# Two moves in a hand-ordered attention and GLU kernel: the last two memory reads of a segment, and the second-half query relays of the first segment

## The chip, the cores and the metric

The kernel runs on one core of one Trainium2 chip. A core has five engines that run side by side and meet through semaphores: TensorE (PE, matmuls; PEld is its weight loader), VectorE (DVE), ScalarE (ACT), GpSimd (POOL) and SyncE (SP), which here only issues transfers. Transfers run on 16 DMA engines. Matmul results go to PSUM, a small memory from which DVE or ACT must copy them out; POOL can't read it.

The metric is device time in microseconds (us), the median of three runs. One execution was also profiled; its trace gives every instruction's start and length.

## The reference

An input x of 2048 rows by 640 columns is normalized by rows. One branch is attention with 32 heads of 20 columns in four segments of 512 rows. Inside a segment it is causal softmax attention; a memory M of all segments before it is read with phi(q) and then updated with phi(k) and v. The other branch is a gated feed-forward layer. The result is x + s * silu(feed-forward).

```python
xn = _layernorm(x, axis=-1)
for s in range(N):                       # N = 4 segments of L = 512 rows
    logits = einsum('bhqd,bhkd->bhqk', qs, ks) * scale + mask
    a_dot = einsum('bhqk,bhkd->bhqd', softmax(logits), vs)
    pq = phi(qs)
    num = einsum('bhld,bhde->bhle', pq, M)
    den = einsum('bhld,bhd->bhl', pq, z)[..., None] + 1e-06
    o = g * (num / den) + (1.0 - g) * a_dot
    pk = phi(ks)
    M = M + einsum('bhld,bhle->bhde', pk, vs)
    z = z + einsum('bhld->bhd', pk)
s = concat(o) @ wo
h = sigmoid(xn @ w_gate) * (xn @ w_up)
return x + s * silu(h @ w_down)
```

## The kernel before

**Segments and slots.** After a start-up part, the kernel goes through the four segments. A segment has 20 slots: 4 pairs of head groups by 5 units of score tiles. A slot begins with its score matmuls (`scores`, L522, into Sps); ACT turns them into weights pt by an exponential over 128 x 2048 (L527), POOL masks the diagonal (L530), and a slot or two later PE multiplies pt with the values (`weigh`, L547, into Aps). Between these fixed pieces PE gets other work: the value, key and query products of the next segment (`v_tile` L360, `k_chunk` L289, `q_chunk` L321), the gate, up and down products (L428, L438, L456), the output product of the segment before (`o_proj`, L502), the memory update (`m_update`, L388) and the memory reads.

**A planner at build time.** All engines' orders are written out by this Python code; nothing is reordered later. `at(time, cost, fn)` puts a task into a heap, due at a time counted in slots, with a planned PE cost in us. A task of a cost over 0.1 goes to `tasks`, others to `soft`. Each slot has two fills: the first runs tasks that are due before now + 0.45, the second tasks and soft work due before now + 1.0. In both, feed-forward work (`bulk`) is handed out as far as the slot's budget goes, which is a common level less the planned costs of the tasks in the slot. R is 20/24 = 0.833 slots, a unit of many due times; w is the first slot of a segment.

**PSUM tiles.** Everything on PE but scores and attention output takes its PSUM tile from one pool, `ps_d`, with three tiles. A matmul group can begin when the tile that it takes over has been copied out by DVE or ACT.

**A memory read** (`mem_read`, L402 to L420) is three matmuls from phi(q) in q5 and the memory in Mbd into a tile am (L410), and then three DVE steps that empty it: the denominator (L415, rm), its reciprocal (L417) and the product into om (L418). There are eight in each segment from the second on: row block `i // 2` by column half `i % 2`. They are due from L671, the memory's update of the same segment from L664.

**Transfers and SP's queue.** SP issues its transfers in the recorded order and waits in place for what each needs. Their completions are counted on eight semaphores in turn, so that a transfer also waits until the eighth before it has landed. Queries and keys of a segment are first written out to DRAM (Qs, Ks) and then *relayed* back in the layout of the scores, head by head (`relay`, L274, four transfers for a half of the heads, into KT and QT). The *bound* of the logits, Cs, goes the same way into four more rows of QT (`c_in`, L353, four transfers for a half). The second half of the heads is first used in slot 10. In the first segment these relays are recorded in the start-up part (L630 to L632). There too the planner gets the normalization of the next segment's last two row blocks (`ln_norm`, L626 and L627: DVE makes xn, and SP transposes it into xnT by a transfer, L263). Value products with these blocks are due from slot 5 on (L649). Phi of the keys is transposed by SP into pkt (L378), which the memory update reads.

Of the kernel before, what the change touches and what calls it, by code (L numbers as in the profile page):

```python
# [55 lines left out]
R = NSLOT / 24  # L56
# [3 lines left out]
def kernel(  # L60
# [30 lines left out]
    Qs = [dpool.tile([D, L], BF, name=f"Qs{i}") for i in range(2)]  # L91
# [11 lines left out]
    def at(time, cost, fn, *a):  # L103
        count[0] += 1
        heapq.heappush(first if fn is phi else tasks if cost > 0.1 else soft, (time, count[0], cost, fn, a))
# [80 lines left out]
    QT = [cpool.tile([P, 4, L], BF, name=f"QT{i}") for i in range(3)]  # L186
# [5 lines left out]
    def v_ones(a, b):  # L192
        for i in range(a, b):
            nc.gpsimd.memset(V[i][:, :, DH:VW], 1.0)
# [32 lines left out]
    def ln_stats(n, p, i0=0, i1=2):  # L227
        s = st[n]
        x = s[f"x{p}"]
        if i0 == 0:  # L230
            s[f"mv{p}"] = lnp.tile([P, 2, 2], F32, name="mv")
            s[f"rstd{p}"] = lnp.tile([P, 2], F32, name="rstd")
        mv, rstd = s[f"mv{p}"], s[f"rstd{p}"]
        for i in range(i0, i1):
            bs = lnp.tile([P, 2, 6], F32, name="bs")
            nc.vector.bn_stats(bs[:, 0, :], x[:, i, 0:HB])
            nc.vector.bn_stats(bs[:, 1, :], x[:, i, HB:D])
            nc.vector.bn_aggr(mv[:, i, :], bs[:])

        def root():  # L240
            nc.gpsimd.tensor_scalar(rstd[:, i0:i1], mv[:, i0:i1, 1], EPS, None, op0=ALU.add)
            nc.gpsimd.tensor_tensor(rstd[:, i0:i1], rstd[:, i0:i1], nhalf[:, i0:i1], op=ALU.pow)
        if n <= 1:
            root()
        else:
            later(0.6, root)

    def ln_norm(n, p, i):
        s = st[n]
        if "xnT" not in s:  # L250
            s["xnT"] = xpool.tile([P, DC, L], BF, name="xnT")
        xn = lnp.tile([P, D], BF, name="xn")
        nc.vector.tensor_scalar(xn[:], s[f"x{p}"][:, i, :], s[f"mv{p}"][:, i, 0:1], s[f"rstd{p}"][:, i:i + 1],
                                op0=ALU.subtract, op1=ALU.mult)
        j = 2 * p + i
        dst = s["xnT"][:, :, j * P:(j + 1) * P]
        if n == 0:
            pT = dtile([P, DC, P], BF, "pT")
            for c in range(DC):
                nc.tensor.transpose(pT[:, c, :], xn[:, c * P:(c + 1) * P], ident[:])  # L260
            nc.scalar.copy(dst, pT[:])
        elif n == 1:
            nc.sync.dma_start_transpose(dst, xn[:])  # L263
        else:
            later(0.7, lambda: nc.sync.dma_start_transpose(dst, xn[:]))


    def half_tile(tiles, n, half):
        return tiles[(2 * n + half) % 3]

    def relay(n, half, src, dst):
        rows = src[n % 2].rearrange("(g r d) n -> r d g n", r=4, d=DH)
        for r in range(4):
            nc.sync.dma_start(half_tile(dst, n, half)[32 * r:32 * r + DH, :, :], rows[r][:, 4 * half:4 * half + 4, :])  # L274
# [33 lines left out]
    def stage_out(n, half, src, dst, name):  # L308
        a, b = ((0, 3), (3, 5))[half]
        nc.sync.dma_start(src[n % 2][a * P:b * P, :].rearrange("(c p) n -> p c n", p=P), st[n][name][:, a:b, :])  # L310
        if n:
            later(1.0, relay, n, half, src, dst)
# [36 lines left out]
    def c_in(n, halves=(0, 1)):  # L349
        rows = Cs[n % 2].rearrange("b (g r) n -> r b g n", r=4)  # L350
        for half in halves:
            for r in range(4):
                nc.sync.dma_start(half_tile(QT, n, half)[32 * r + DH:32 * r + KR, :, :],  # L353
                                  rows[r][:, 4 * half:4 * half + 4, :])

    def v_tile(n, j, half):
        s = st[n]
        ps = dtile([P, HB], F32, "psv")
        for k in range(DC):
            nc.tensor.matmul(ps[:], lhsT=s["xnT"][:, k, j * P:(j + 1) * P],  # L360
                             rhs=W["v"][:, k, half * HB:(half + 1) * HB],
                             start=(k == 0), stop=(k == DC - 1))
        va = V[4 * (n % 2) + j]
        evacuate(va[:, half * 16:(half + 1) * 16, 0:DH], ps[:].rearrange("p (h e) -> p h e", e=DH))
# [203 lines left out]
    def warm(count):  # L568
        ps = dtile([P, L], F32, "wps")
        for i in range(count):  # L570
            nc.tensor.matmul(ps[:, 0:P], lhsT=ident[:], rhs=ident[:], start=True, stop=True)

    def startup():
        warm(WARM)
        nc.gpsimd.memset(KT[0][:], 1.0)
        ln_stats(0, 0, 0, 1)
        ln_stats(0, 0, 1, 2)
        ln_norm(0, 0, 0)
        warm(10)
        ln_stats(0, 1, 0, 1)  # L580
        ln_norm(0, 0, 1)
        v_tile(0, 0, 0)
        ln_stats(0, 1, 1, 2)
        v_tile(0, 1, 0)
        ln_norm(0, 1, 0)
        v_tile(0, 0, 1)
        ln_norm(0, 1, 1)
        v_tile(0, 2, 0)
        v_tile(0, 1, 1)
        v_tile(0, 2, 1)  # L590
        v_ones(0, 4)
        make_ind()
        nc.gpsimd.memset(KT[1][:], 1.0)
        for c in range(DC):
            k_chunk(0, c)
        nc.gpsimd.memset(KT[2][:], 1.0)
        stage_out(0, 0, Ks, KT, "k5")
        for c in range(DC):
            q_chunk(0, c)
            if c == 0:  # L600
                stage_out(0, 1, Ks, KT, "k5")
                relay(0, 0, Ks, KT)
            elif c == 2:
                stage_out(0, 0, Qs, QT, "q5")
            if c < 2:
                ln_stats(1, 0, c, c + 1)
        make_bd()
        v_ones(4, 8)
        take(1)
        q_bound(0)  # L610
        relay(0, 0, Qs, QT)
        stage_out(0, 1, Qs, QT, "q5")
        c_in(0, (0,))
        load_glu(1, 0)
        load_glu(1, 1)
        ln_stats(1, 1, 0, 1)
        gates()
        take(1)
        ln_norm(1, 0, 0)
        ln_norm(1, 0, 1)  # L620
        take(1)
        ln_stats(1, 1, 1, 2)
        take(5)
        at(0.1, 0.68, v_tile, 0, 3, 0)
        at(0.5, 0.68, v_tile, 0, 3, 1)
        at(R * 2.0, 0.0, ln_norm, 1, 1, 0)  # L626
        at(R * 2.3, 0.0, ln_norm, 1, 1, 1)  # L627
        load_glu(2, 0)
        load_glu(2, 1)
        relay(0, 1, Ks, KT)  # L630
        relay(0, 1, Qs, QT)
        c_in(0, (1,))  # L632

    startup()
    at(7.5, 0, load_late, "d", B_w_down)
# [3 lines left out]
    for n in range(NSEG):  # L639
        w = NSLOT * n  # L640
        m = n + 1
        if m < NSEG:
            if n:
                for p in range(2):
                    for i in range(2):
                        at(w + (-1.4, -0.7, 0.1, 0.55)[2 * p + i], 0.1, ln_stats, m, p, i, i + 1)
                        at(w + (0.6, 0.9, 1.7, 2.0)[2 * p + i], 0.1, ln_norm, m, p, i)
            for i in range(8):
                at(w + R * (3.5 + (0.6 * i if i < 4 else 2.5 + 0.55 * (i - 4))), 0.68, v_tile, m, i // 2, i % 2)  # L649
            for c in range(DC):  # L650
                at(w + R * (8.8 + 1.0 * c if n else 9.4 + 0.9 * c), 1.08, k_chunk, m, c)
                at(w + R * (13.8 + 1.1 * c), 1.08, q_chunk, m, c)
                if m + 1 < NSEG:
                    at(w + R * (12.8 + 0.85 * c), 0.0, phi, m, "k5", c)
                at(w + R * (17.4 + 0.8 * c), 0.0, phi, m, "q5", c)
            at(w + R * 19.2, 0.6, q_bound, m)
            if m + 1 < NSEG:
                for p in range(2):
                    at(w + R * (16.1 + p), 0.0, x_load, m + 1, p)
            if n == 0:  # L660
                for c in range(DC):
                    at(R * (2.6 + 0.8 * c), 0.0, phi, 0, "k5", c)
            for i, cs in enumerate(([0, 1, 2], [3, 4])):
                at(w + (9.05, 11.0)[i], 0.75 - 0.25 * i, m_update, n, cs)  # L664
        if n >= 1:
            for j in range(4):
                at(w + R * (1.1 + 0.3 * j), 0.0, o_ready, n - 1, j)
                at(w + R * (4.0 + 0.5 * j if j < 3 else 9.6), 0.0, xr_load, n - 1, j)
            for i in range(8):
                at(w + R * (5.4 + 1.1 * i), 0.68, o_proj, n - 1, i // 2, i % 2)  # L670
                at(w + R * (3.4 + 0.85 * i), 0.25, mem_read, n, i // 2, i % 2)  # L671

    for j in range(4):
        at(NSLOT * NSEG - 8 + 0.5 * j, 0.0, xr_load, NSEG - 1, j)
# [71 lines left out]
    n = NSEG - 1  # L746
# [39 lines left out]
```

## Time and profile before

| What | us |
|---|---|
| median of three runs | 339.26 |
| lowest and highest of them | 338.82, 339.61 |
| the profiled execution | 337.32 |
| its span, from first to last instruction | 335.6 |
| mean granted TensorE clock in it | 1.0 of full speed |

| Work | How often | Busy us | Mean ns |
|---|---|---|---|
| exponential of the scores, ACT L527 | 80 | 150.1 | 1876 |
| mask, POOL L530 | 80 | 77.1 | 963 |
| gate matmuls, PE L428 | 240 | 59.6 | 379 |
| up matmuls, PE L438 | 240 | 59.7 | 379 |
| down matmuls, PE L456 | 384 | 57.1 | 299 |
| attention output, PE L547 | 1280 | 44.5 | 173 |
| output product, PE L502 | 160 | 25.9 | 300 |

The profiled execution gives every duration used below; the time of a run holds a little more than the span. Busy time is no measure of what sets the end: an engine that is off the chain may idle or be busy at no cost. The matmuls' ends are modelled, so that they seem to overlap; the time from the start of one group of matmuls to the start of the next is the better measure. In a timeline a line is a group of instructions: its start, its length, engine, line, operation, what it writes and reads, how many; in brackets the idle time of that engine ahead of it and who ended it.

### The profile page before, as it was taken

Reading aid. Unit: us, or ns where it says so; the run is one execution under the profiler, and the core shown is the slowest. Engines: PE = TensorE matmul, PEld = TensorE weight load, DVE = VectorE, ACT = ScalarE, POOL = GpSimd, SP = SyncE. Lnnn points to the kernel's source line nnn. Section 1 sums busy time; section 2 is a strip of 40 time slices with the busy share of each in tenths; the row PEclk is TensorE's granted clock in tenths of the full one; section 3 lists DMA queues with packets and bytes.
Section 4 is the critical chain, followed back from the end, with each engine's and each line's share of the span. In section 5 each row is a group of like instructions: output and inputs, shape, how many; then the busy total and the mean of one; then the engine's idle time right before and its main releaser. Section 6 shows DMA issues by size and latency. Waiting matters only on the chain.

```text
span 335.6 us, 8361 instructions
## 1 busy us (share of the span) xinstructions
PE 328.0 (98%) x3402; PEld 186.1 (55%) x3402; DVE 224.0 (67%) x532; ACT 226.1 (67%) x237; POOL 111.6 (33%) x157
## 2 busy tenths in 40 slices
PE   7999999999999999999999999999999999999995
PEld 6544455555664565644565466554556665544673
DVE  6376366589868677688756978885663687543365
ACT  3653897788876675477686775566887776786730
POOL 6645222323236222332233523242222323223214
PEclk9999999999999999999999999999999999999999
DMA  7956984674811621135620461142220620210032
GB/s 234 328 196 198 288 105 85 230 226 117 205 57 36 123 80 41 49 117 120 189 72 2 61 142 56 47 152 68 72 70 3 93 76 32 76 43 3 2 62 78
DMA packets 54725, 35.53 MB, mean 106 GB/s; under 512 B 28576, under 2 KB 54688, under 8 KB 54688
## 3 DMA queue, kind: packets, MB, share of 16 engines
q1 hardware_dynamic: 52480, 32.23, 37.0%
q10 hardware_dynamic: 2208, 2.79, 2.4%
q8 instruction: 26, 0.43, 0.5%
q14 instruction: 11, 0.09, 0.1%
HBM read 20.19 MB, written 8.39 MB: 85 GB/s over the span
## 4 chain that ended last, share of the span: by engine, by line
PE 86%; DMA 6%; DVE 3%; ACT 2%; SPq 1%; issue 1%; DVEq 0%
PE yp L456 15%; PE up L438 14%; PE gp L428 14%; PE Aps L547 9%; PE Sps L522 7%; PE sp L502 7%; PE psk L289 6%; PE psv L360 6%; PE psq L321 5%; DMA Wu<-in_B_w_up_dram 2%; DMA Ks<-k 2%; DMA xnT<-xn 1%; PE dm L388 1%; ACT pt L527 1%; PE am L410 1%; DMA Qs<-q 1%
## 5 line engine op out<-in xcount | busy, mean ns | idle before, releaser
L527 ACT ACTIVATE pt<-Sps 128x2048 bf16<-128x2048 f32 x80 | 150.1, 1876 | 27.2 <-PE Sps L522 25.1
L530 POOL TENSOR_SCALAR_AFFINE_SELECT pt<-pt 128x1024 bf16<-128x1024 bf16 (+1 forms) x80 | 77.1, 963 | 197.0 <-ACT pt L527 197.0
L428 PE MATMUL gp<-xnT,Wg 128*128 128x512 bf16 x240 | 59.6, 379 | 0.4 <-DVE om L418 0.3
L438 PE MATMUL up<-xnT,Wu 128*128 128x512 bf16 x240 | 59.7, 379 | 0.3 <-DMA Wu<-in_B_w_up_dram 0.3
L456 PE MATMUL yp<-Wd,hT 128*128 128x320 bf16 x384 | 57.1, 299 | 0.0
L442 DVE SCALAR_TENSOR_TENSOR hT<-tg,up 128x512 bf16<-128x512 bf16 x48 | 32.7, 682 | 36.0 <-PE up L438 34.1
L547 PEld LDWEIGHTS <-pt 128*128 128x128 bf16 x1280 | 43.2, 96 | 14.3 <-issue 1.1
L431 ACT ACTIVATE tg<-gp 128x512 bf16<-128x512 f32 x48 | 28.6, 596 | 29.2 <-PE gp L428 26.9
L547 PE MATMUL Aps<-va,pt 128*128 128x21 bf16 x1280 | 44.5, 173 | 0.0
L456 PEld LDWEIGHTS <-hT 128*128 128x128 bf16 x384 | 35.4, 97 | 15.2 <-issue 2.4
L438 PEld LDWEIGHTS <-Wu 128*128 128x128 bf16 x240 | 21.2, 97 | 23.8 <-issue 2.6
L461 DVE SCALAR_TENSOR_TENSOR aa<-t,yp 128x320 bf16<-128x320 bf16 x32 | 15.5, 484 | 27.6 <-ACT t L459 27.5
L428 PEld LDWEIGHTS <-Wg 128*128 128x128 bf16 x240 | 21.0, 97 | 21.7 <-issue 1.7
L522 PE MATMUL Sps<-QT,KT 24*128 24x128 bf16 (+3 forms) x512 | 31.9, 301 | 0.2
L459 ACT ACTIVATE t<-yp 128x320 bf16<-128x320 f32 x32 | 14.0, 437 | 19.9 <-PE yp L456 18.8
L360 PE MATMUL psv<-Wv,xnT 128*128 128x320 bf16 x160 | 26.4, 299 | 0.4 <-DMA xnT<-xn 0.3
L502 PE MATMUL sp<-Wo,oT 128*128 128x320 bf16 x160 | 25.9, 300 | 0.3 <-DVE om L418 0.3
L321 PE MATMUL psq<-xnT,Wq 128*128 128x512 bf16 x100 | 24.3, 380 | 0.0
L289 PE MATMUL psk<-xnT,Wk 128*128 128x512 bf16 x100 | 24.2, 379 | 0.0
L522 PEld LDWEIGHTS <-KT 24*128 24x128 bf16 x512 | 9.2, 92 | 24.7 <-issue 23.4
L504 DVE SCALAR_TENSOR_TENSOR aa<-aa,sp 128x320 bf16<-128x320 bf16 x32 | 15.5, 484 | 8.2 <-PE sp L502 8.0
L502 PEld LDWEIGHTS <-oT 128*128 128x128 bf16 x160 | 14.5, 98 | 8.3 <-issue 2.0
(74 smaller groups left out, 325.9 us busy)
## 6 DMA issues: line engine op xcount, KB each, us to landing
KT<-Ks SPq DMA_DIRECT2D x32, 80.0 KB
QT<-Qs SPq DMA_DIRECT2D x32, 80.0 KB
xr<-in_A_x_dram SPq DMA_DIRECT2D x15, 160.0 KB
out_dram<-xr SPq DMA_DIRECT2D x15, 160.0 KB
xt<-in_A_x_dram SPq DMA_DIRECT2D x6, 320.0 KB
Wg<-in_B_w_gate_dram SPq DMA_DIRECT2D x3, 640.0 KB
Wu<-in_B_w_up_dram SPq DMA_DIRECT2D x3, 640.0 KB
Wd<-in_B_w_down_dram ACTq DMA_DIRECT2D x1, 1920.0 KB
```

Source lines behind the costliest of these rows:

```text
L289: nc.tensor.matmul(ps[:], lhsT=W["k"][:, k, c * P:(c + 1) * P], rhs=s["xnT"][:, k, :], start=(k == 0), stop=(k == DC - 1))
L321: nc.tensor.matmul(ps[:], lhsT=W["q"][:, k, c * P:(c + 1) * P], rhs=s["xnT"][:, k, :], start=(k == 0), stop=(k == DC - 1))
L360: nc.tensor.matmul(ps[:], lhsT=s["xnT"][:, k, j * P:(j + 1) * P], rhs=W["v"][:, k, half * HB:(half + 1) * HB], start=(k == 0), stop=(k == ...
L428: nc.tensor.matmul(gp[:], lhsT=Wg[f // 4][:, k, fo:fo + P], rhs=s["xnT"][:, k, :], start=(k == 0), stop=(k == DC - 1))
L438: nc.tensor.matmul(ps[:], lhsT=Wu[f // 4][:, k, fo:fo + P], rhs=s["xnT"][:, k, :], start=(k == 0), stop=(k == DC - 1))
L442: empty(lambda: nc.vector.scalar_tensor_tensor(out=h[:], in0=tg[:], scalar=1.0, in1=ps[:], op0=ALU.add, op1=ALU.mult))
L456: nc.tensor.matmul(yp[:], lhsT=s["hT"][f][:, j * P:(j + 1) * P], rhs=W["d"][:, f, hs], start=(f == 0), stop=(f == FC - 1))
L502: nc.tensor.matmul(sp[:], lhsT=s["oT"][:, j, c, :], rhs=W["o"][:, c, hs], start=(c == 0), stop=(c == DC - 1))
L522: nc.tensor.matmul(Sps[:, r, c0:c0 + ncol], lhsT=kt[32 * r:32 * r + KR, gi, kb * P:(kb + 1) * P], rhs=qt[32 * r:32 * r + KR, gi, kb * P:L] ...
L527: nc.scalar.activation(pt[:], Sps[:], ACT.Exp, scale=SCALE)
L530: nc.gpsimd.affine_select(out=diag, in_=diag, compare_op=ALU.is_ge, fill=0.0, base=0, pattern=[[0, 4], [0, cnt], [1, P]], channel_multipli ...
L547: nc.tensor.matmul(A[:, qb, r, :], lhsT=pt[:, r, off:off + P], rhs=V[4 * (n % 2) + kb][:, 4 * g + r, :], start=first, stop=True, skip_grou ...
```

## The change

Two edits. The due time of a segment's seventh and eighth memory reads (i = 6 and 7) changes from `w + R * (3.4 + 0.85 * i)`, which is 7.08 and 7.79 slots into the segment, to `w + i + 1.55`, which is 7.55 and 8.55. And the second-half relays of Q and of the bound in the first segment are no longer issued where the start-up part ends, but given to the planner, due at 2.17 and 2.25 slots; the two normalizations are due at 1.67 and 1.92. All four are soft work.

```diff
         load_glu(2, 0)
         load_glu(2, 1)
         relay(0, 1, Ks, KT)
-        relay(0, 1, Qs, QT)
-        c_in(0, (1,))
+        at(R * 2.6, 0.0, relay, 0, 1, Qs, QT)
+        at(R * 2.7, 0.0, c_in, 0, (1,))
...
                 at(w + R * (5.4 + 1.1 * i), 0.68, o_proj, n - 1, i // 2, i % 2)
-                at(w + R * (3.4 + 0.85 * i), 0.25, mem_read, n, i // 2, i % 2)
+                at(w + (R * (3.4 + 0.85 * i) if i < 6 else i + 1.55), 0.25, mem_read, n, i // 2, i % 2)
```

## The prediction

> **What bounds the kernel now.** I read the busy shares and the chain that ended last first, then the waits, then timelines of three places.
>
> ```profile
> PE 328.0 (98%) x3402; PEld 186.1 (55%) x3402; DVE 224.0 (67%) x532; ACT 226.1 (67%) x237; POOL 111.6 (33%) x157
> ...
> PE 86%; DMA 6%; DVE 3%; ACT 2%; SPq 1%; issue 1%; DVEq 0%
> ```
>
> TensorE (PE) sets the end: busy 98% of the span, 86% of the chain. Both kernels give it the same matmuls, so only its waits can change the time. The view of waits gives, per engine and line, who was waited for, us in total, times and the longest. PEld, the loader of PE's weights, often pauses because PE is full ("issue"); it waits for others here:
>
> ```profile
> PEld L438 <- DMA Wu<-in_B_w_up_dram: 0.6, 1, 0.6
> PEld L360 <- DMA xnT<-xn: 0.6, 1, 0.6
> PEld L428 <- DVE om L418: 0.5, 1, 0.5
> PEld L502 <- DVE om L418: 0.5, 1, 0.5
> ```
>
> The first, a weight transfer of the start-up, is not touched. The other three are at 50.3, 128.3 and 207.3 us. (A fourth of 0.4 us, of a memory read itself on L418 at 276.4 us, lies ahead of the moved reads and stays.) Timeline of segment 0 (start, length, engine, line; in brackets idle time and who ended it):
>
> ```profile
> 38.09 5.77 SPq L274 DMA_DIRECT2D QT<-Qs  x4
> ...
> 38.31 1.49 DVE L253 TENSOR_SCALAR xn<-xt,mv,rstd 128x640 bf16<-128x640 bf16 x2
> ...
> 43.91 1.34 SPq L353 DMA_DIRECT2D QT<-Cs  x4
> ...
> 45.34 2.53 SPq L263 DMA_TRANSPOSE xnT<-xn  x2
> ...
> 49.65 0.39 PE L522 MATMUL Sps<-QT,KT 24*128 24x512 bf16 x4
> ...
> 50.35 0.85 PE L360 MATMUL psv<-Wv,xnT 128*128 128x320 bf16 x5 [0.31 <-DMA xnT<-xn]
> ...
> 52.90 0.40 PE L522 MATMUL Sps<-QT,KT 24*128 24x128 bf16 x8
> ...
> 53.22 0.85 PE L360 MATMUL psv<-Wv,xnT 128*128 128x320 bf16 x5
> ```
>
> The normalized rows xn are ready at 39.80, but SP is in its eight relays until 45.25, so their transposes start 5.5 us late and the value matmuls wait. From scores to value matmuls takes 0.32 us where nothing waits (52.90 to 53.22) and 0.70 here: **0.38 us lost**.
>
> Timeline of segment 2, slots 6 and 7:
>
> ```profile
> 206.27 0.40 PE L522 MATMUL Sps<-QT,KT 24*128 24x256 bf16 x8
> 206.60 0.34 PE L410 MATMUL am<-Mbd,q 128*128 128x147 bf16 x3
> 207.26 0.85 PE L502 MATMUL sp<-Wo,oT 128*128 128x320 bf16 x5 [0.32 <-DVE om L418]
> ...
> 209.44 0.33 PE L410 MATMUL am<-Mbd,q 128*128 128x84 bf16 x3
> 209.61 1.24 PE L428 MATMUL gp<-xnT,Wg 128*128 128x512 bf16 x5
> ```
>
> The seventh read follows the sixth (205.62) with only attention matmuls between. A read is 0.17 us of PE (209.44 to 209.61), but holds one of three PSUM tiles until three DVE steps are done. The next matmul group needs the sixth read's tile; its om ends at 206.72 + 0.49 = 207.21, so the group starts at 207.26 instead of 206.77: **0.49 us lost**. Segment 1 has the same picture: read at 127.63, om until 128.23, gp at 128.29, again 0.66 - 0.17 = **0.49 us**. Segment 3 has up, 1.08 us, between sixth and seventh read and loses nothing there.
>
> **The change, part by part.** Nothing is added or removed. In recorded order the seventh read leaves the first half of slot 7 for its second half (due 7.08, now 7.55) and the eighth goes from slot 7 to the second half of slot 8 (7.79, now 8.55). Because their 0.25 of planned cost moves too, the planner shifts one gate or up group of feed-forward work in segments 1 and 2. Further off, no matmul changes place.
>
> *Adjacency.* Each neighbouring pair of groups has its own start-to-start time. In segment 2 the pairs that vanish are scores-read 0.33, read-sp 0.17, sp-psk 0.69, read-gp 0.17, gp-scores 1.17, up-scores 1.17: 3.70. Those that appear are scores-sp 0.33, sp-gp 0.69, gp-psk 1.08, read-scores 0.26, up-read 1.09, read-scores 0.25: 3.70. Segment 1 comes out even at 3.44, segment 3 within 0.05. Cost nothing.
>
> *The wait removed.* In segment 2 sp now takes the seventh read's place at 206.60; the tile it reuses is that of the value copy, done at about 206.32. gp follows at 207.29, when om (207.21) is just over. Gain 0.49; segment 1 likewise (sp 127.63, gp 128.32 against 128.23). Together **-0.98**. The hand-over of 0.05 after om (207.21 to 207.26) still fits in both.
>
> *Where the stall could go.* The reads' DVE steps (0.20 + 0.28 + 0.41 from start to start) now stand later on DVE. In segment 2, with every PE start taken 0.49 earlier: sp ends 207.29, its aa runs at 207.72, xr at 208.2, the key copy (psk ends 209.46) at 209.66, the seventh read's om from 210.74; up needs its tile at 212.43, over one us later. In slot 8: od 213.4, hT 213.81 to 214.49 (dm needs it at 215.19), the eighth read's om 214.89 to 215.38 (sp after dm needs it at 216.00), the maximum over keys, then the key copy 215.9 to 216.59 (psk needs it at 217.28). So 0.57 us of cover is the least I find. Segment 1 by the same working keeps about as much, segment 3 more (DVE idles 0.6 to 0.7 us before each hT). If the cover were gone, one wait costs what DVE is late, up to the three steps' 0.89 us in each segment. Bounds: 0 to 3 x 0.89 = 2.67; I take 0. The Mbd update by POOL comes after dm and stays behind the last read: the eighth read's matmuls (213.52) lie 1.7 us before dm (215.19).
>
> *The relays.* SP's order becomes key relays, two transposes, four QT relays, four bound relays, then the pkt transposes. SP is free at 38.05, xn's first half at about 39.06, second at 39.80: the transposes issue at 39.1 and 40.4 (1.22 to 1.30 us each). Landing: at best 4.96 us after issue, as at 45.34, so 44.1. At worst, from the pair issued at 30.76 with two weight transfers in flight: the first QT relay reuses that transpose's completion semaphore and was issued at 38.09, so it had landed within 7.3 us; that gives 46.4. PE wants it at 49.97, the second half at 51.7 (40.4 + 7.3 = 47.7). Covered at both ends, gain **-0.38**. On SP's one queue the waiting transposes hold back the relays by at most 1.1 us (38.05 to 39.1); after them the relays still stand behind the same weight transfers, whose landing let the third and fourth QT relay go at 40.82 and 43.59. The last two bound relays now wait for the transposes' completions (by 47.7), and then pkt comes, as before at 47.97. QT's second half is first read at slot 10 (66 us), pkt at 63.78: at least 8 us of cover for five transposes that took 7.85 us to issue, up to 55.8. Cost nothing.
>
> The Trainium skill, in "DMA: Bandwidth & Descriptors" (Queues, rings and completion order), says that each DMA engine consumes one issuer's descriptors in ring order. By that rule our transposes would stand behind the last weight transfer, landed by 43.59; with 4.96 behind it they would land at 48.6, and the sum stays, with 1.4 us of margin in place of 3.6. No run shown has this order of the two, so it only feeds the first rival's chance.
>
> *Sum.* -0.98 - 0.38 = **-1.36 us**. The profiled execution took 337.32 (span 335.6 and 1.72 around it): 335.96, span 334.2. The three runs shown have a median 1.94 above that execution; waits of this kind are fixed lengths, so 339.26 - 1.36 = **337.9**. Everything behind a removed wait is released by PE itself and moves up; no later wait of PE on a DMA is in the view of waits.
>
> **Rivals.**
> 1. *Transposes late anyway.* The DMA share is above 1 from 32 to 40 us (309 to 315 GB/s). If the two weight transfers and the transposes slow each other past 49.97, the 0.38 stays: 338.3. Against it: 3.6 us of margin by rows.
> 2. *The read wait changes owner.* Another PSUM tile is late by as much where the reads now stand, and only the start-up gains: 338.9. For it: three tiles only, and xr took 1.04 at 209.13 against 0.49 to 0.56 elsewhere, beside a POOL mask; a hit of 0.5 is nearly the least cover above.
> 3. *Slower: DVE falls behind in slot 8.* There it now has od, hT, the read's three steps, the maximum and the key copy in a row before the matmul group after dm. If DVE is later than my 0.57 us of cover, PE waits at sp or psk in each segment; above 0.45 a segment (1.36 / 3) the change loses, at the full 0.89 it is 339.26 - 1.36 + 2.67 = 340.6. Against it: DVE is 67% busy, and before the change the key copy in slot 8 waits for its matmuls.
> 4. *Absorbed.* A later wait that does not follow PE takes the time back: 339.2. Against it: the late waits are short and on engines that PE feeds. That the edit does not do what it says is excluded: the recorded order shows all moves.
>
> **Numbers.** Forecast 0.62; rivals 0.12, 0.13, 0.08, 0.05. A measurement here tells 0.2% (0.68 us) from no change: the runs spread 0.8. Faster by more means below 338.58: the forecast nearly whole (0.58) and about two thirds of rival 1 (0.08): 0.66. Within: rivals 2 and 4 and the rest of these: 0.26. Slower, above 339.94: 0.08. Range: from 337.3 (the forecast less 0.6, for the spread and in case earlier transposes free more) to 339.4 (rivals 1, 2 and 4 within).
>
> **What would show it.** In the new profile: transposes of xnT at 39 to 42 us and no wait of L360 on them; no wait of L428 or L502 on om; 0.32 and 0.17 us pairs at these places; a span near 334.2. Wrong if PE waits on L278's copy, on L418 or L399 in slots 7 to 9, or if the first transposes land after 50 us.

## The result

| | Before | Changed |
|---|---|---|
| median of six runs, us | 338.94 | 337.21 |
| lowest and highest | 338.28, 339.61 | 335.73, 337.50 |
| the profiled execution | 337.32 | 337.24 |
| its span | 335.6 | 335.5 |

The ratio is 0.9955 with a 95% interval of 0.9939 to 0.9971: 0.45% faster, 1.5 us. Laid on the 339.26 that the prediction started from, that is 337.7, against 337.9 forecast; the six runs' own median is 0.1 below the range's low end. In ten later runs of the same kernel the ratio was 0.9966 (0.9949 to 0.9984), which is 338.1 on the same footing. A ratio leaves out a run over 1.5% above the fastest of its kernel, which is one run of q_early below (341.11 us).

One thing is odd at once: the two profiled executions have the same span. The one before is the unusual one: its 337.32 lies below all six timed runs of its kernel, while 337.24 lies inside the changed kernel's six. The first lines of the changed kernel's page, busy time and the chain that ended last, look much as before, but for 3% of the chain that went from DMA to DVE:

```profile
PE 328.2 (98%) x3402; PEld 187.0 (56%) x3402; DVE 223.1 (66%) x532; ACT 226.2 (67%) x237; POOL 111.4 (33%) x157
...
PE 85%; DVE 6%; DMA 3%; ACT 2%; issue 1%; SPq 1%; POOL 0%; DVEq 0%; ACTq 0%; POOLq 0%
```

The view of waits of the changed kernel (us in total, times, the longest) no longer has PE or its loader wait for xnT, nor L428 and L502 for om. Others have grown or are new: the second gate and up weights, and od ahead of L547 (0.9 before on PEld):

```profile
PEld L547 <- DVE od L556: 1.3, 3, 0.7
...
PEld L438 <- DMA Wu<-in_B_w_up_dram: 1.0, 1, 1.0
...
PE up L438 <- DMA Wu<-in_B_w_up_dram: 0.7, 1, 0.7
...
PEld L428 <- DMA Wg<-in_B_w_gate_dram: 0.5, 1, 0.5
...
PE Aps L547 <- DVE od L556: 0.4, 1, 0.4
```

The start of the changed kernel's timeline answers to the first place shown of before:

```profile
37.09 1.25 PE L438 MATMUL up<-xnT,Wu 128*128 128x512 bf16 x5 [0.72 <-DMA Wu<-in_B_w_up_dram]
...
39.82 2.52 SPq L263 DMA_TRANSPOSE xnT<-xn  x2
42.39 3.93 SPq L274 DMA_DIRECT2D QT<-Qs  x4
46.36 1.34 SPq L353 DMA_DIRECT2D QT<-Cs  x4
...
50.39 0.39 PE L522 MATMUL Sps<-QT,KT 24*128 24x512 bf16 x4
50.72 0.85 PE L360 MATMUL psv<-Wv,xnT 128*128 128x320 bf16 x5
```

The transposes go ahead of the eight relays, and scores to value matmuls take 0.33 us (50.39 to 50.72) in place of 0.70. But up, at 37.09, had lost 0.72 to its weights, 0.4 more than before, and the gate group ahead of it (34.79) came 0.3 us later behind its value matmuls than before. Segment 2, the second place:

```profile
206.77 0.40 PE L522 MATMUL Sps<-QT,KT 24*128 24x256 bf16 x8
207.10 0.85 PE L502 MATMUL sp<-Wo,oT 128*128 128x320 bf16 x5
207.79 1.24 PE L428 MATMUL gp<-xnT,Wg 128*128 128x512 bf16 x5
...
210.36 0.33 PE L410 MATMUL am<-Mbd,q 128*128 128x147 bf16 x3
```

sp and gp follow without a gap, and the seventh read comes at 210.36.

To see where time goes I compare when the score matmuls of each of the 80 slots start. For each profile, the difference to the profile before is taken at the ends of a stretch; the table gives by how much it changes in the stretch (us, plus is a loss). Segments 0 to 3 begin at slots 0, 20, 40 and 60; kernels further down are the experiments.

| Kernel | up to slot 2 | 2 to 6 (value matmuls) | 17 to 21 | 27 to 30 (reads, seg. 1) | 47 to 50 (reads, seg. 2) | 67 to 70 (reads, seg. 3) | all 80 |
|---|---|---|---|---|---|---|---|
| changed | +0.74 | -0.38 | +0.62 | -0.50 | -0.50 | -0.07 | -0.07 |
| changed, again | +0.36 | -0.39 | -0.01 | -0.49 | -0.51 | -0.07 | -1.10 |
| relays_only | -0.28 | -0.38 | +0.55 | +0.01 | -0.01 | 0.00 | -0.08 |
| reads_only | +1.03 | -0.21 | +0.55 | -0.49 | -0.51 | -0.07 | +0.30 |
| seventh_only | +0.69 | -0.29 | +0.69 | -0.49 | -0.49 | -0.06 | +0.05 |
| eighth_only | +0.64 | -0.20 | +1.19 | 0.00 | -0.02 | -0.06 | +1.56 |
| bound_only | +0.20 | -0.38 | +0.56 | +0.01 | 0.00 | 0.00 | +0.40 |
| dve_two | +0.96 | -0.38 | +0.69 | +0.08 | +0.14 | -0.06 | +1.43 |
| value_first | +0.63 | +2.98 | +0.68 | -0.49 | -0.50 | -0.07 | +3.22 |
| late_store | -0.36 | -0.38 | +0.56 | -0.49 | -0.50 | -0.07 | -1.26 |
| q_early | -0.20 | -0.38 | +0.69 | -0.49 | -0.50 | -0.07 | -0.96 |
| q_first_early | +0.03 | -0.38 | -0.01 | -0.49 | -0.51 | -0.07 | -1.41 |

Outside these six stretches no profile differs from before by more than 0.03 us in sum. At the four places that the change touches it gains 0.38 + 0.50 + 0.50 + 0.07 = 1.45 us. The two stretches that it doesn't touch took 1.36 back in this one execution.

### The profile page after: what moved, and what is told of

It is laid out like the page before. It is cut to its first block, busy times and chain, and to the rows that moved or that the text cites. A ratio compares the mean times of both kernels' runs of the same rounds, so it can differ in the third digit from the quotient of the medians.

```text
span 335.5 us, 8363 instructions
## 1 busy us (share of the span) xinstructions
PE 328.2 (98%) x3402; PEld 187.0 (56%) x3402; DVE 223.1 (66%) x532; ACT 226.2 (67%) x237; POOL 111.4 (33%) x157
## 4 chain that ended last, share of the span: by engine, by line
PE 85%; DVE 6%; DMA 3%; ACT 2%; issue 1%; SPq 1%; POOL 0%; DVEq 0%; ACTq 0%; POOLq 0%
PE up L438 14%; PE gp L428 14%; PE yp L456 12%; PE Aps L547 9%; PE Sps L522 7%; PE sp L502 7%; PE psk L289 7%; PE psv L360 6%; PE psq L321 5%; DMA Wu<-in_B_w_up_dram 2%; PE wps L571 2%; PE dm L388 1%; PE am L410 1%; DMA Qs<-q 1%; DVE q L374 1%
## 5 line engine op out<-in xcount | busy, mean ns | idle before, releaser
L428 PE MATMUL gp<-xnT,Wg 128*128 128x512 bf16 x240 | 59.6, 379 | 0.2
L547 PEld LDWEIGHTS <-pt 128*128 128x128 bf16 x1280 | 43.2, 96 | 14.7 <-DVE od L556 1.3
L547 PE MATMUL Aps<-va,pt 128*128 128x21 bf16 x1280 | 44.5, 173 | 0.4 <-DVE od L556 0.4
L428 PEld LDWEIGHTS <-Wg 128*128 128x128 bf16 x240 | 21.0, 97 | 21.8 <-issue 1.7
L502 PE MATMUL sp<-Wo,oT 128*128 128x320 bf16 x160 | 25.9, 300 | 0.0
L502 PEld LDWEIGHTS <-oT 128*128 128x128 bf16 x160 | 14.4, 97 | 8.2 <-issue 2.6
```

The costliest lines, as they stand in the source:

```text
L428: nc.tensor.matmul(gp[:], lhsT=Wg[f // 4][:, k, fo:fo + P], rhs=s["xnT"][:, k, :], start=(k == 0), stop=(k == DC - 1))
L502: nc.tensor.matmul(sp[:], lhsT=s["oT"][:, j, c, :], rhs=W["o"][:, c, hs], start=(c == 0), stop=(c == DC - 1))
L547: nc.tensor.matmul(A[:, qb, r, :], lhsT=pt[:, r, off:off + P], rhs=V[4 * (n % 2) + kb][:, 4 * g + r, :], start=first, stop=True, skip_grou ...
```

## The experiments

Each was timed in runs of its own beside the kernel before; value_first ran once.

**relays_only: the moved relays, with the reads where they were.**

```diff
-        relay(0, 1, Qs, QT)
-        c_in(0, (1,))
+        at(R * 2.6, 0.0, relay, 0, 1, Qs, QT)
+        at(R * 2.7, 0.0, c_in, 0, (1,))
```

> Only the relays' part of the change; the memory reads stand where they stood. Theory: the value matmuls of the third row block no longer wait for xnT (the 0.38 us at 50 us is gone: 0.32 us from scores to value matmuls), the waits of 0.49 us on om in segments 1 and 2 stay. 0.38 us less, ratio to the kernel before about 0.999. Rival (the transposes are held up by the weight transfers anyway): the wait on xnT stays at 0.3 us or more, ratio 1.000.

Ratio 0.9989 (0.9970 to 1.0008). The profile has no wait of PE on xnT, and both waits on om. The table's row has -0.38 at the value matmuls and nothing at the reads. The theory holds in the profile; the times alone could not tell it from none.

**reads_only: the moved reads, with the relays where they were.**

```diff
-                at(w + R * (3.4 + 0.85 * i), 0.25, mem_read, n, i // 2, i % 2)
+                at(w + (R * (3.4 + 0.85 * i) if i < 6 else i + 1.55), 0.25, mem_read, n, i // 2, i % 2)
```

> Only the memory reads' part; the relays stand ahead of the transposes as before. Theory: both waits of 0.49 us on om in segments 1 and 2 are gone and no new one comes; the 0.38 us on xnT stays. 0.98 to 1.05 us less, ratio about 0.997. Rival (the wait changes owner): PE waits for another PSUM tile in slots 7 to 9, ratio 0.999 to 1.000.

Ratio 0.9947 (0.9927 to 0.9966): nearly all of the change's gain, and more than the sum of waits says (0.997), which the interval excludes narrowly; what the rest is stays open. Places: -0.49 and -0.51, and no new wait in slots 7 to 9. The wait for xnT stayed, but at 0.17 us (50.68 to 51.17 is 0.49, less the 0.32 of a free passage) and not 0.38:

```profile
50.68 0.39 PE L522 MATMUL Sps<-QT,KT 24*128 24x512 bf16 x4
51.17 0.85 PE L360 MATMUL psv<-Wv,xnT 128*128 128x320 bf16 x5
```

PE came 1.03 us later here, after a slower start-up, but the transposes issued 1.02 us later too (46.36 against 45.34). The wait is shorter because the first transpose landed sooner behind its issue: 4.76 us, against 4.96 before (start of the value matmuls, less the hand-over of 0.05). In seventh_only and eighth_only 0.09 and 0.18 are left, with 4.49 and 4.74.

**seventh_only and eighth_only: one of the two reads.**

```diff
# seventh_only
+                at(w + (R * (3.4 + 0.85 * i) if i != 6 else i + 1.55), 0.25, mem_read, n, i // 2, i % 2)
# eighth_only
+                at(w + (R * (3.4 + 0.85 * i) if i < 7 else i + 1.55), 0.25, mem_read, n, i // 2, i % 2)
```

> Of the two reads only the seventh moves (due 7.55), the eighth keeps 7.79; relays as before. Theory: the wait belongs to the pair of sixth and seventh read, so this alone takes both waits of 0.49 us away and the eighth's move is worth nothing: ratio about 0.997, no wait on om in segments 1 and 2, though seventh and eighth read now stand close together in slot 7. Rival (the eighth had to make room): with both reads in the second half of slot 7 a matmul group behind them waits on om for up to 0.5 us in each segment, and the ratio stays at 0.999 to 1.000.

> Of the two reads only the eighth moves (due 8.55), the seventh keeps 7.08; relays as before. Theory: sixth and seventh read stay neighbours, the group behind them waits 0.49 us on om in segments 1 and 2, so nothing is gained: ratio 1.000, within 0.1%. Rival (room in slot 7 is what pays): ratio 0.998 or less.

seventh_only: ratio 0.9959 (0.9943 to 0.9975), both waits gone, -0.49 and -0.49. Its timeline in segment 1 shows seventh and eighth read side by side, six matmuls in 0.43 us, and the group behind them does not wait:

```profile
131.99 0.49 PE L410 MATMUL am<-Mbd,q 128*128 128x147 bf16 x6
132.42 0.39 PE L522 MATMUL Sps<-QT,KT 24*128 24x512 bf16 x4
132.74 1.25 PE L289 MATMUL psk<-xnT,Wk 128*128 128x512 bf16 x5
```

eighth_only keeps both waits; in segment 2 the read is at 208.25 and gp 0.66 behind it, as before:

```profile
208.25 0.34 PE L410 MATMUL am<-Mbd,q 128*128 128x147 bf16 x3
208.91 1.25 PE L428 MATMUL gp<-xnT,Wg 128*128 128x512 bf16 x5 [0.32 <-DVE om L418]
```

So the pair of sixth and seventh read was the whole matter, and the eighth's move is worth nothing at those places. The time of eighth_only is not that clean: 0.9978 (0.9960 to 0.9997), 0.75 us less where its places show 0.08. That is the number of the rival, though the places do not show its mechanism. Its profiled execution was the longest of its six runs and has two large losses elsewhere (+0.64, +1.19). The spread of those stretches from one execution to the next is large enough for that, but I have not shown that it is the cause.

**bound_only: only the bound's relays behind the transposes.**

```diff
         relay(0, 1, Qs, QT)
-        c_in(0, (1,))
+        at(R * 2.7, 0.0, c_in, 0, (1,))
```

> Of the relays only the four of the bound go behind the transposes; Q's four stay ahead, and so do the reads' old places. The transposes then issue when the fourth relay of Q has gone, which waits for a weight transfer: at about 43.9 us of the profile before instead of 45.3, or of 39 to 40 with the whole change. Theory (a margin of 3 us or more behind the early transposes): issued at 43.9 they land up to 4.96 later, at 48.9, still ahead of the 49.97 at which the value matmuls want them, so the wait on xnT is gone here too and Q's relays needn't have moved: 0.38 us less, ratio 0.999. Rival (transposes need the head start): a wait on xnT of 0.1 to 0.4 us stays.

SP's queue and PE in this kernel's timeline:

```profile
37.94 6.10 SPq L274 DMA_DIRECT2D QT<-Qs  x4
44.13 2.52 SPq L263 DMA_TRANSPOSE xnT<-xn  x2
46.70 1.50 SPq L353 DMA_DIRECT2D QT<-Cs  x4
...
49.85 0.39 PE L522 MATMUL Sps<-QT,KT 24*128 24x512 bf16 x4
50.17 0.85 PE L360 MATMUL psv<-Wv,xnT 128*128 128x320 bf16 x5
```

Issued at 44.13, the transposes are in time: 0.32 from scores to value matmuls. 1.2 us of head start were enough in this execution, and Q's relays needn't have moved for it. The ratio, 0.9998 (0.9979 to 1.0017), can't show 0.1%.

**value_first: when do the early transposes land?** The value products of the next segment take the third row block first.

```diff
-                at(..., 0.68, v_tile, m, i // 2, i % 2)
+                at(..., 0.68, v_tile, m, (i // 2, (2, 0, 1, 3)[i // 2])[n == 0], i % 2)
```

> The changed kernel with segment 0's value products of the next segment in another order of row blocks: the third (the first that needs the moved transposes) is taken first, at about 42.7 us, so that PE waits for it and shows when the first transpose has landed. By the rows: 39.8 + 4.96 = 44.8 at best, and 47.0 at worst, where a relay that waits for the same completion had gone. Theory of free passage: 44.8 or earlier, PE waits 2 us. Rival (ring order behind the weight transfer, whose completion let a relay go at 45.28): 45.3 or later, PE waits 2.6 us or more. The wait is lost: the run is 1.5 to 4 us longer than the changed kernel.

One execution, 340.53 us. SP's queue in short windows and PE's timeline:

```profile
40.17 2.52 SPq L263 DMA_TRANSPOSE xnT<-xn  x2
...
45.16 1.04 SPq L274 DMA_DIRECT2D QT<-Qs  x3
...
45.90 0.85 PE L360 MATMUL psv<-Wv,xnT 128*128 128x320 bf16 x5 [3.19 <-DMA xnT<-xn]
```

PE starts at 45.90, so the first transpose landed about 5.7 us after its issue. The second relay of Q, which waits for the weight transfer, went at 45.16, 0.7 us ahead. That is the rival's side: issued during the transfer, the transpose did not overtake it. Whether it stood behind the transfer or was only slowed by it, one execution can't tell.

**dve_two: how much cover is there behind the eighth read?** The changed kernel with two more DVE steps in front of the eighth read's three, whose results are not used.

```diff
+        [nc.vector.scalar_tensor_tensor(out=s["aq"][:, k, :], in0=W["q"][:, 0, 0:L], scalar=1.0,
+            in1=W["q"][:, 1, 0:L], op0=ALU.min, op1=ALU.max) for k in range(2 if (j, b) == (3, 1) else 0)]
         nc.vector.scalar_tensor_tensor(out=rm[:], in0=am[:, :, DH], scalar=1e-6, ...
```

> The changed kernel with two more DVE steps ahead of the eighth read's three in each segment: a minimum and maximum over 128x512, 0.69 us each and 0.60 from start to start (their result is not used). It measures the cover that the prediction worked out, 0.57 us, and the rival that DVE falls behind in slot 8. Theory: DVE is 1.2 us later there, so the output product after dm waits for om 1.2 - 0.57 = 0.6 us in segments 1 and 2, with nothing in segment 3: 1.2 us more than the changed kernel, about 338.4. If the cover is much larger: no wait. If it is near nothing: 1.2 us in each, 2.4 more or worse.

Ratio to the kernel before 0.9994 (0.9979 to 1.0009), median 338.37. Segment 2, PE and DVE:

```profile
215.73 1.28 DVE L414 SCALAR_TENSOR_TENSOR aq<-Wq 128x512 bf16<-128x512 bf16 x2
...
217.42 0.49 DVE L418 TENSOR_TENSOR om<-am,rm 128x320 bf16<-128x320 f32 x1
...
217.97 0.85 PE L502 MATMUL sp<-Wo,oT 128*128 128x320 bf16 x5 [0.47 <-DVE om L418]
```

sp starts 0.06 after om ends (217.91). Against the changed kernel's rows this costs 0.58 in segment 1 (+0.08 for -0.50) and 0.64 in segment 2, and 0.01 in segment 3: 1.2 us, as expected. The cover is real and no larger than worked out.

**late_store, q_early, q_first_early: two losses that the change left.** In the start-up, PE waits for the second gate and up weights. late_store puts the store of Q's second half, which the late relays no longer need early, behind that transfer:

```diff
-        stage_out(0, 1, Qs, QT, "q5")
         c_in(0, (0,))
         load_glu(1, 0)
         load_glu(1, 1)
+        stage_out(0, 1, Qs, QT, "q5")
```

> The changed kernel, with the store of Q's second half (256 KB, and 0.4 us of SP) behind the second pair of weight transfers instead of ahead of it; the relays that read it now come later anyway. Theory: the first up group that needs the second up weights waits for that transfer 0.3 to 0.7 us in all profiles so far (at 36 to 37 us); the transfer issues 0.4 us earlier and with 256 KB less ahead of it, so this wait falls by 0.4 us or more: ratio 0.994 to the kernel before. Rival (a smaller transfer ahead changes nothing, or the first relays are held up in turn): ratio 0.9955 as the changed kernel.

Ratio 0.9935 (0.9918 to 0.9952), median 336.16. In its timeline the up group now follows the scores by 0.35 us, where the changed kernel took 1.12 (35.97 to 37.09) and before 0.72:

```profile
35.63 0.40 PE L522 MATMUL Sps<-QT,KT 24*128 24x128 bf16 x8
35.98 1.25 PE L438 MATMUL up<-xnT,Wu 128*128 128x512 bf16 x5
```

Of the two kernels below, which keep the late store, q_first_early has 0.36 there too, but in q_early PE waited again (0.69). From slot 0 to slot 2 these three take 5.9 to 6.2 us, the ten other profiles 6.3 to 7.6.

The other loss, in slots 17 to 21, is in nine of the first ten profiles; only before's has none. The changed kernel's DVE and POOL at that point, and PE further on:

```profile
88.66 0.30 DVE L373 TENSOR_SCALAR q<-q 128x512 bf16<-128x512 bf16 x1 [0.43 <-DMA Qs<-q]
88.99 0.69 DVE L374 SCALAR_TENSOR_TENSOR q<-ex,q 128x512 bf16<-128x512 bf16 x1
89.60 0.29 DVE L373 TENSOR_SCALAR q<-q 128x512 bf16<-128x512 bf16 x1
89.67 1.17 POOL L530 TENSOR_SCALAR_AFFINE_SELECT pt<-pt 128x1024 bf16<-128x1024 bf16 x1 [3.43 <-ACT pt L527]
89.92 1.47 DVE L374 SCALAR_TENSOR_TENSOR q<-ex,q 128x512 bf16<-128x512 bf16 x1
...
98.62 0.76 PE L547 MATMUL Aps<-va,pt 128*128 128x21 bf16 x24 [0.40 <-DVE od L556]
```

phi of a query chunk is written in place, so it waits until the store of the first three chunks has read them: 0.43 us. That makes the second chunk's L374 start behind POOL's mask, and it takes 1.47 in place of 0.69. DVE stays late from there on, od too, and at 98.62 the attention matmuls wait for it, which is 0.47 of the loss. In the profile before, that L374 began 0.12 us ahead of the mask, and took its 0.69:

```profile
89.18 0.69 DVE L374 SCALAR_TENSOR_TENSOR q<-ex,q 128x512 bf16<-128x512 bf16 x1
...
89.30 1.53 POOL L530 TENSOR_SCALAR_AFFINE_SELECT pt<-pt 128x1024 bf16<-128x1024 bf16 x1 [3.43 <-ACT pt L527]
```

On top of late_store, q_early issues both stores of Q earlier in each segment, q_first_early only the first:

```diff
-            later(0.9, stage_out, n, c // 4, Qs, QT, "q5")
+            later(0.7, stage_out, n, c // 4, Qs, QT, "q5")                      # q_early
+            later(0.7 if c == 2 else 0.9, stage_out, n, c // 4, Qs, QT, "q5")   # q_first_early
```

> The late store's kernel with the stores of Q issued 0.17 slots earlier in every segment, which puts the first store ahead of one transpose of pkt in SP's queue. In eight of nine profiles the phi step on the first query chunk waits 0.2 to 0.9 us for that store (DVE L373 on Qs), and one or two DVE steps behind it then run beside POOL's mask at 1.2 to 1.6 us in place of 0.3 to 0.7; PE loses 0.5 to 0.65 us at 93 to 100 us. The profile before, alone, has none of this and is 2 us shorter than its kernel's median. Theory: the store leaves 1.2 us earlier, the phi step waits for ACT alone and starts ahead of the mask, the loss of 0.5 us goes: 0.15% less than the late store, ratio 0.992. Rival (the DVE step meets the mask anyway, since ACT's exponential sets both): no wait on Qs, but the long L374 at 89 us stays, ratio 0.9935.

> As the early store of Q, but only its first store (three of five chunks) goes ahead of a transpose of pkt; the second keeps its place, so that the bound's store is no longer behind four relays of Q, which cost a wait of the scores on QT of 0.66 us in the profile of the early store. Theory: both waits are gone, the phi step on Qs and the scores on QT: 0.5 us less than the late store, ratio 0.992. Rival (differences this small are lost in the start-up's spread): no wait in the profile, but a ratio within 0.992 to 0.995 that the interval can't tell from the late store's 0.9935.

q_early: ratio 0.9931 (0.9910 to 0.9951). The wait on Qs and the long step at 88 us are gone (0.69), but slots 17 to 21 lose 0.69 all the same. The view of waits names a new owner: the bound's store now stands behind four relays of Q, and the scores wait for it.

```profile
PE Sps L522 <- DMA QT<-Cs: 0.3, 1, 0.3
```

q_first_early: neither wait, -0.01 in slots 17 to 21, the lowest median of all, 335.71, and ratio 0.9934 (0.9908 to 0.9960). That is the rival of its expectation: gone in the profile, not to be told from late_store in time.

**after_again: the changed kernel once more.**

> The changed kernel once more, in the same runs as the early store of Q. Theory: the three removed waits stay away (no wait of PE on xnT, none of L428 and L502 on om); the wait of PE on the second up weights at 37 us and the loss at 93 to 100 us come back in other sizes, as they did in most profiles. Ratio 0.9955, between 0.994 and 0.997.

Ratio 0.9966 (0.9949 to 0.9984), median 337.30 of ten runs. Its profile is the second row of the table: the same gains of 0.39, 0.49 and 0.51, with +0.36 in the start-up. The loss in slots 17 to 21, which the expectation had come back, is not there. Its span is 334.5.

## Why the prediction was right, point by point

- *What bounds the kernel.* Right: only PE's waits moved the time, and outside six stretches nothing moved.
- *The wait removed at the reads, 0.49 each.* Right: 0.50 and 0.50, in every kernel that moves the seventh read (dve_two then loses it again in slot 9), in none that doesn't. That segment 3 comes out even was 0.07 us off, in the change's favour.
- *Where the stall could go, 0.57 us of cover.* Right in place and size. In the changed kernel's segment 2, om ends at 215.85 and sp starts at 216.49, 0.59 later with the hand-over of 0.05 taken off; dve_two filled the cover with 1.2 us of DVE and paid 0.58 and 0.64. Rivals 2 and 3 fall with it.
- *The relays, 0.38.* Right in that execution's terms, and mis-sized as an average. The wait that it removes was 0.38 only in the profile before; with the relays where they were, the three other profiles have 0.17, 0.09 and 0.18, depending on how the landing falls against PE's arrival. The part of the change that is sure is the reads.
- *Transposes land by 46.4 at the latest.* 45.9 in value_first, within the bounds; 5.7 us behind the issue there, between 4.96 and 7.3. The 4.96 was not "at best", as three other profiles have 4.5 to 4.8, but PE's margin did not hang on it. Ring order, as the Trainium skill has it in "DMA: Bandwidth & Descriptors" (Queues, rings and completion order), agrees with that run, 0.7 us behind the weight transfer; the 4.96 that I added by the rule was too much. Rival 1 falls: PE wanted them four us later.
- *Moved reads and relays cost nothing else.* Right: outside the six stretches nothing differs by more than 0.03, so rival 4 has no place where the gain is taken back. That the loss in slots 17 to 21 belongs to the change is not borne out: kernels with either half alone have it, and the changed kernel's second profile has not.
- *The profile to expect: a span near 334.2.* Wrong for the execution that was shown (335.5), near for the second one (334.5). The step that failed is "The profiled execution took 337.32 (span 335.6 and 1.72 around it): 335.96, span 334.2": it took every untouched wait to come back as in one execution, though that one lay 1.94 below the median of the runs. It did not ask what the 1.94 was. About 0.6 of it is most likely the loss in slots 17 to 21, which nine of the eleven profiles with the stores of Q at their old due time have; the kernel before was profiled only once, so this is not shown for it. The start-up differs by -0.3 to +1.0 among the profiles that share it. What the rest is stays open. The forecast in absolute time held because the gains are differences at places that these two don't touch. That the two ratios put it so close, 337.7 and 338.1 around 337.9, is luck in part: their intervals are 1.1 to 1.2 us wide.

## What to carry to other kernels

Cost a reordering by the waits that it removes, and measure the cover behind its new place in the same view; here that was good to a tenth of a us. When two profiles show no difference and the times do, compare them place by place, start against start, before believing either: one execution's luck at an untouched place can be as large as the whole change. A step that writes in place has a reader to wait for; moving that reader's transfer is cheap, as long as what is queued behind it is not needed soon.

## What was not expected of the hardware

L374 is a DVE step on bf16 tiles in SBUF. It takes 0.69 us alone; in the eight profiles in which it started at 88 to 94 us just behind the start of POOL's mask, it took 1.46 to 1.63, so it seems to have waited for most of the mask. In the changed kernel's profile it took 1.47 when it started 0.25 us into the mask (which ended at 90.84, 0.55 us before the step did); in the profile before, where it started 0.12 us ahead of the mask, it kept 0.69, and the mask took 1.53 in place of some 1.1. The Trainium skill, in "SBUF — State Buffer" (Terms), has the two engines share one port pair, which the loser waits for; these rows agree.
